# Capped attention and a rational MLP on one core: the row sums of four head pairs made together, tanh written from PSUM to SBUF, and another order of the products

## The chip, the cores and the metric

The kernel runs on one core of a Trainium2 chip. The metric is the device time of one execution in microseconds (us). The time before is 669.54 us, the median of three runs (669.12 to 669.55). A measurement of this kernel can tell a change of about 0.2% (1.3 us) from none.

## The reference

Attention with capped scores over 4 batches, 12 heads, 448 positions and a head dimension of 64, then an MLP whose activation is a rational function, all in float32:

```python
scores = q @ k.T / sqrt(64)
scores = cap * tanh(scores / cap)                       # cap = 30
attn = exp(scores - max(scores)); attn /= sum(attn) + 1e-9
x = (attn @ v)                                          # [1792, 768] over all heads
h = x @ w_in                                            # [1792, 2048]
P = a0 + a1*h + a2*h**2 + a3*h**3
Q = 1 + |b0|*|h| + |b1|*h**2
out = (P / (Q + 1e-6)) @ w_out                          # [1792, 768]
```

With a cap of at most 40 the kernel takes no maximum: the exponent is bounded (`self.bounded` is true here, and only this branch runs).

## The kernel before

**Attention.** The 48 heads are worked as 24 pairs, p = 0 to 23. The scores stand transposed, keys on the partitions and 448 queries in the free dimension. A pair has three full tiles of 128 keys, n = 0 to 2, each with both heads side by side (128 x 896); the last 64 keys of an even pair and of the odd pair behind it share a fourth tile, n = 3, which is made with the odd pair. So two pairs have seven tiles. Each tile is made by three products of split operands (`scores`, L417) into one of three pairs of PSUM banks (`PS`, in the order rows ps_127, ps_128, ps_129). ScalarE then takes tanh in place in PSUM (`softmax`, L429) and exp from PSUM to a tile in SBUF (`exp`, L447). There are six such SBUF tiles for n = 0 to 2 (`etiles`) and two for n = 3. VectorE adds the three exp tiles of a pair into one tile (`es`, L453, four buffers).

Then TensorE makes, per pair, the products with V (`pv`, L501, into the PSUM bank pv for even pairs and mi for odd ones), and per two pairs the products of the shared tile (`pv_tails`, L518) and the row sums (`norm`, L546). `norm` multiplies `es` and the n = 3 tile by columns of ones. Each of its products gives 32 rows of the result, so four of them lie side by side in the array: two rounds of four, into mi. VectorE copies the sums out (L550), four small DMAs fold them, VectorE takes reciprocals (L559, L560), one DMA writes them to DRAM and two DMAs spread them over 64 partitions. VectorE multiplies the output of each pair by them (`xout`, L579). All these DMAs go through GpSimd's queue, those of the last two `norm`s through SyncE's.

Before a pair's scores its keys and queries are transposed on TensorE (`prep_k`, L338 and L340, `prep_q`, L361), and VectorE (in the first pair ScalarE too) splits them out of PSUM with four instructions (L345, L346, L376, L379). This is done two pairs ahead.

**MLP.** `stage1` (L803, then L788) multiplies x by a block of w_in, `rational` (L834 to L847) works on ScalarE and VectorE, `stage2` (L873) multiplies by w_out. x is split into two parts (`split_x`, L590 and L591), half of it while attention still runs and half of it behind.

**The order.** Nothing runs in program order as such: `op` records each piece of work with a cost, the keys that it reads and writes, and a priority, and `Plan.flush` places them by these costs into one fixed order per engine. On the chip every engine then follows its own order and waits on semaphores. `visits(p)` gives the program order of a pair's pieces, which sets the priorities:

```python
            if p == 0:
                return [s0, s1, s2, (k, 1), (q, 1)]
            if p == 1:
                return [s0, s1, (k, 2), s2, t, (q, 2), (pv, 0), (k, 3), (q, 3)]
            if not p % 2:
                return [s0, s1, s2, (pv, p - 1), (tails, p - 1), *new]
            sums = (norm, p // 2 - 1)
            if p == P1 - 1:
                return [s0, s1, (pv, p - 1), sums, s2, t]
            return [s0, s1, (pv, p - 1), s2, t, *new, sums]
```

Here s0 to s2 and t are `scores` and `softmax` of the tiles, and `new` is the transposing for pair p + 2. The text calls TensorE's work on consecutive tiles of scores a scores block, the transposes of a pair a transpose block, and two pairs' work (from one odd pair's V block to the next) a period.

Of the kernel before, what the change touches and what calls it, by code (L numbers as in the profile page):

```python
# [22 lines left out]
RING, ARENA_F, ARENA_R = 3072, 15104, 24576  # L23
NE = 6
X_AT, RING_V32 = 5376, 2816
# [19 lines left out]
WARM2 = (2, 1, 3)  # L45
Q_ACT = ()
# [7 lines left out]
E_SC = 0  # L54
SC_NS = 615
# [4 lines left out]
D_NS = 1430  # L60
E_W = 10
# [181 lines left out]
class Body:  # L243
# [151 lines left out]

    def slot(self, p, n):

        return (1, 2, 0, 1)[n] if p % 2 else n
# [42 lines left out]
    def exp(self, p, n, src, sk, e, ek):  # L441
# [9 lines left out]
        es, ks = self.es[p % 4], [("es", p % 4)]  # L451
# [76 lines left out]
    def norm(self, k):  # L528
# [7 lines left out]
        DB, sc, dn = self.DB, self.SC[k % 2], self.dn[k % 2]  # L536
        es = [self.es[(2 * k + x) % 4] for x in range(2)]
# [11 lines left out]
        self.op(PE, D_NS + SHAPE_NS, sums, [("es", (2 * k + x) % 4) for x in range(2)] + [tk, "ones"], [dk, "turn"])  # L549
# [19 lines left out]

    def last_norm(self, k):  # L570

        return k + 1 == self.B * self.NP // 2
# [9 lines left out]
    def split_x(self, m, kc):  # L582

        nc = self.nc
        XH, XL = (t[m][kc].rearrange("p (b t) -> p b t", b=2) for t in (self.XH, self.XL))
# [7 lines left out]
    def attention(self):  # L593
# [7 lines left out]
        for t, x in [(self.ones, 1.0)] + [(self.half[j][64 * y:64 * y + 64], float(j == y)) for j in range(2) for y in range(2)]:  # L601
# [9 lines left out]
        def norm(k):  # L611
            self.norm(k)
            todo.extend([None] * (1 - len(todo)) + [2 * k, 2 * k + 1])

# [6 lines left out]
        def visits(p):  # L621
# [19 lines left out]
            return [s0, s1, (pv, p - 1), s2, t, *new, sums]  # L641
# [128 lines left out]
    def stage1(self, u, between=None):  # L770
# [10 lines left out]
        if between:  # L781
            for x, ts in enumerate(parts):
                def run(ts=ts):
                    w = wi().rearrange("p s (k f) -> p s k f", f=128)
                    for kc in range(KC):
                        h, lo = (t[m][kc][:, ts] for t in (self.XH, self.XL))
# [9 lines left out]
        for kc in range(KC):  # L796
            h, lo = ([t[m][kc][:, ts] for ts in parts] for t in (self.XH, self.XL))
# [180 lines left out]
    def memory(self):  # L978
# [42 lines left out]
        for l, nm, num, w in ((self.es, "es", 4, 896),):  # L1021
            for n in range(num):
                t, o = take(w)
                keys("A", o, ((nm, n), w))
                l.append(t.rearrange("p (a b) -> p a b", b=448))
# [9 lines left out]
        t, o = take(96)  # L1035
        keys("A", o, ("ones", 96))
        self.ones, *self.half = (t[:, 32 * x:32 * x + 32] for x in range(3))
        for n in range(2):
            t, o = take(56, 32)
# [59 lines left out]

        base[0] = ARENA_R - 3 * 896  # L1100
# [12 lines left out]
        for m in range(2):  # L1113
            for kc in range(self.KC):
                for l, nm in ((self.XH, "xh"), (self.XL, "xl")):
                    t, o = take(2 * self.S, dt=F32R)
                    keys("M", o, ((nm, m, kc), 2 * self.S))
                    l[m].append(t)
# [4 lines left out]
        for n, at, l, name in ((0, 0, self.wi, "w_in"), (0, 1, self.wi, "w_in"), (1, 0, self.wi, "w_in"), (1, 1, self.wo, "w_out")):  # L1123
            self.rings[(name, len(l))] = [("rv", n, 0), ("v32", n, 0), ("v32", n, 1)]
            at *= 2 * self.DM
            wt(l, name, 2 * 10 ** 6 + 4 * (RING * n + at), lambda n=n, at=at: self.shared(n)[:, at:at + 2 * self.DM])

# [12 lines left out]
    def run(self):  # L1140
        tc = self.tc
        self.rslot, self.made, self.later = {}, set(), {}
        with ExitStack() as ctx:
# [11 lines left out]
            self.dn = dp.tile([2, 4, self.S], F32, name="dn")  # L1155
            self.gtile = lambda dt: T("etiles", [128, 896 * (NE + 2)], dt)
            self.etiles = self.gtile(F32)
            self.ringtile = lambda n, dt: T(f"ring{n}", [128, RING], dt)
# [14 lines left out]
def attention_rational_mlp(ctx: ExitStack, tc: tile.TileContext, q, k, v, cap, moe_w_in, moe_w_out,  # L1173
# [4 lines left out]
    with tc.manual_schedule():  # L1178
# [21 lines left out]
        for n in (4, 5, 3):  # L1200
# [61 lines left out]
```

## Time and profile before

| | us |
|---|---|
| median of three runs | 669.54 |
| the profiled execution | 666.99 |
| its span, first to last instruction | 665.0 |
| TensorE busy | 652.5 (98%) |
| VectorE busy | 547.0 (82%) |
| ScalarE busy | 442.9 (67%) |
| GpSimd busy | 96.3 (14%) |
| mean granted TensorE clock | 0.998 of full |

The profile is of one execution, and its engines' busy times include the pipelined ends of matmuls, so that TensorE's 98% hides waits that are shorter than such an end. Where a product starts is exact, so the text measures blocks from the start of one to the start of the next. Attention's first scores start at 8.59 us, its last TensorE work ends at 192.39 us; the MLP takes the rest.

### The profile page before, as it was taken

To read this page: it belongs to the slowest core of one execution; us is meant where nothing else is said; L and a number is where in the kernel's file an instruction comes from. 1 tells how busy PE (TensorE), PEld (TensorE's weight loads), DVE (VectorE), ACT (ScalarE), POOL (GpSimd) and SP (SyncE) were. 2 spreads that over 40 slices of the span, in tenths; PEclk is the share of its full clock that TensorE was granted. 3 is DMA by queue.
4 is the path that set the end of the run, shared out by engine and by line. 5 is a ranking of instruction groups with operands and counts; after the bars stand their busy time and mean duration, and the time that the engine had idled before them with its cause. 6 is when DMAs were issued, how large, how long until landed. Compare 5 with 4: busy or idle time off the path is not lost.

```text
span 665.0 us, 9868 instructions
## 1 busy us (share of the span) xinstructions
PE 652.5 (98%) x3852; PEld 541.4 (81%) x3852; DVE 547.0 (82%) x677; ACT 442.9 (67%) x531; POOL 96.3 (14%) x159
## 2 busy tenths in 40 slices
PE   7999999999999999999999999999999999999996
PEld 4555555555458899999999999999999999999996
DVE  4779899998959988887996996899699789959753
ACT  5798989998958866765576455657645665754460
POOL 4023323323200000021012002101200210110030
PEclk9999999999999999999999999999999999999999
DMA  7746766764131332276148316714831671482086
GB/s 176 177 125 168 163 159 159 148 131 108 35 106 29 118 143 70 72 143 130 41 92 178 84 49 119 143 50 89 178 87 48 123 139 52 88 174 44 1 138 200
DMA packets 79895, 74.44 MB, mean 112 GB/s; under 512 B 49376, under 2 KB 68064, under 8 KB 79840
## 3 DMA queue, kind: packets, MB, share of 16 engines
q1 hardware_dynamic: 68240, 48.68, 26.1%
q0 software_dynamic: 10448, 24.80, 22.4%
q8 instruction: 32, 0.52, 0.3%
q10 hardware_dynamic: 1152, 0.25, 0.2%
q14 instruction: 23, 0.19, 0.1%
HBM read 47.98 MB, written 25.65 MB: 111 GB/s over the span
## 4 chain that ended last, share of the span: by engine, by line
PE 86%; ACT 6%; DVE 3%; DMA 2%; issue 1%; SPq 0%; ACTq 0%; DVEq 0%
PE ps L788 31%; PE ps L873 17%; PE mi L873 9%; PE pv L873 9%; PE ps L417 8%; PE mi L501 4%; PE pv L501 3%; ACT etiles L447 2%; PE mi L546 2%; ACT ps L429 2%; PE ps L338 1%; PE pv L518 1%; PE ps L361 1%; ACT arena_r L590 1%; DMA arena_f<-in_k_dram 1%
## 5 line engine op out<-in xcount | busy, mean ns | idle before, releaser
L788 PE MATMUL ps<-arena_r,ring 128*128 128x512 f32 (+1 forms) x1008 | 210.8, 363 | 0.0
L788 PEld LDWEIGHTS ps<-arena_r,ring 128*128 128x128 f32 x1008 | 182.2, 188 | 19.2
L290 POOL DMA_DIRECT2D out_dram<-arena_f x49 | 42.4, 865 | 418.8 <-ACT arena_f L900 415.2
L873 PE MATMUL ps<-arena_r,etiles 128*128 128x384 f32 x462 | 89.4, 334 | 0.1
L429 ACT ACTIVATE ps<-ps 128x896 f32<-128x896 f32 x84 | 74.3, 907 | 19.3 <-PE ps L417 18.8
L447 ACT ACTIVATE etiles<-ps,acap 128x896 f32<-128x896 f32 x84 | 82.4, 1011 | 1.1
L873 PEld LDWEIGHTS ps<-arena_r,etiles 128*128 128x128 f32 x462 | 80.9, 188 | 0.4 <-ACT arena_f L900 0.4
L873 PE MATMUL mi<-arena_r,etiles 128*128 128x384 f32 x231 | 77.2, 336 | 0.0
L873 PE MATMUL pv<-arena_r,etiles 128*128 128x384 f32 x231 | 77.0, 335 | 0.0
L417 PE MATMUL ps<-arena_r 64*128 64x448 f32 x576 | 70.8, 379 | 4.6 <-DVE arena_r L346 2.0
L417 PEld LDWEIGHTS ps<-arena_r 64*128 64x128 f32 x576 | 50.5, 184 | 29.5 <-ACT etiles L447 6.8
L834 ACT ACTIVATE arena_f<-ps,b 128x896 f32<-128x896 f32 x32 | 32.3, 1009 | 52.2 <-PE ps L788 52.0
L734 ACT ACTIVATE arena_f<-arena_f 128x768 f32<-128x768 f32 x32 | 29.3, 915 | 45.9 <-DMA arena_f<-in_moe_w_out_dram 31.4
L846 ACT CAST etiles<-arena_f 128x896 fp32r<-128x896 f32 x32 | 30.3, 947 | 42.9 <-DVE arena_f L845 42.9
L838 DVE SCALAR_TENSOR_TENSOR arena_f<-arena_f,bab 128x896 f32<-128x896 f32 x32 | 36.8, 1150 | 20.6 <-ACT arena_f L835 20.5
L843 DVE SCALAR_TENSOR_TENSOR arena_f<-arena_f,one 128x896 f32<-128x896 f32 x32 | 36.7, 1148 | 11.3 <-ACT arena_f L841 11.3
L873 PEld LDWEIGHTS pv<-arena_r,etiles 128*128 128x128 f32 x231 | 43.3, 188 | 0.6
L873 PEld LDWEIGHTS mi<-arena_r,etiles 128*128 128x128 f32 x231 | 43.3, 188 | 0.6
L873 PE MATMUL ps<-ring,etiles 128*128 128x384 f32 x210 | 42.0, 334 | 0.0
L847 DVE TENSOR_TENSOR etiles<-arena_f,etiles 128x896 fp32r<-128x896 f32 x32 | 34.8, 1089 | 6.8 <-ACT etiles L846 6.5
L836 ACT ACTIVATE arena_f<-ps,a 128x896 f32<-128x896 f32 x32 | 35.3, 1103 | 3.5 <-DVE arena_f L844 3.5
L873 PEld LDWEIGHTS ps<-ring,etiles 128*128 128x128 f32 x210 | 36.9, 188 | 0.0
(125 smaller groups left out, 1089.5 us busy)
## 6 DMA issues: line engine op xcount, KB each, us to landing
out_dram<-arena_f POOLq DMA_DIRECT2D x49, 384.0 KB, 6.0
arena_f<-in_moe_w_out_dram SPq DMA_DIRECT2D x16, 768.0 KB, 5.2
arena_f<-in_moe_w_in_dram SPq DMA_DIRECT2D x16, 768.0 KB, 4.8
out_dram<-arena_f SPq DMA_DIRECT2D x13, 384.0 KB, 2.6
ring<-in_q_dram SPq DMA_DIRECT2D x44, 112.0 KB, 4.2
arena_r<-dn POOLq DMA_DIRECT2D x20, 224.0 KB, 4.8
ring<-in_k_dram SPq DMA_DIRECT2D x33, 128.0 KB, 4.3
ring<-in_v_dram SPq DMA_DIRECT2D x11, 384.0 KB, 3.9
```

Source lines behind the costliest of these rows:

```text
L290: self.op(eng, (625 if local else 450) if eng == SP else 1050, lambda: e.dma_start(out, in_, **accum), r, w, nbytes=nbytes, **kw)
L417: m = nc.tensor.matmul(self.PS[i][:, j, 0:448], st[r], mv[r], start=y == 0, stop=y == len(ops) - 1)
L429: self.op(ACT, act_ns(896, True), lambda: nc.scalar.activation(ps, ps, AF.Tanh), ["table"], pk)
L447: self.op(ACT, act_ns(size, sk[0][0] == "ps", 1), lambda: nc.scalar.activation(e, src, AF.Exp, scale=acap), sk + ["table"], [ek])
L501: m = nc.tensor.matmul(po[64 * j:64 * j + 64, 0:448], raw["v"][:, 2 * x + j, 64 * c:64 * c + 64], tiles[c][0][:, j], start=c == 0, stop=False)
L788: r = nc.tensor.matmul(po[:, ts], w[:, y, kc], mv, start=kc == 0 and z == 0, stop=kc == KC - 1 and z == 2)
L834: self.op(ACT, act_ns(n, True, 1), lambda: T.activation(Bt, h, AF.Abs, scale=b[:, 0:1]), hk, bk)
L836: self.op(ACT, act_ns(n, True, 2), lambda: T.activation(A, h, AF.Identity, scale=a[:, 3:4], bias=a[:, 2:3]), hk, ak)
L838: self.op(DVE, dve_ns(n, 1), lambda: stt(Bt, C, bab[:, 1:2], Bt, ALU.mult, ALU.add), ck + ["bab"], bk)
L843: self.op(DVE, dve_ns(n, 1), lambda: stt(Bt, Bt, one, C, ALU.add, ALU.mult), ck, bk)
L847: self.op(DVE, dve_ns(n), lambda: V.tensor_tensor(GL(), A, f32(GH()), ALU.subtract), ak + K("gh", ig), K("gl", ig))
L873: r = nc.tensor.matmul(po[n][:, 0:384], st, mv[:, 384 * n:384 * n + 384], start=(y == 0 and x == 0), stop=(y == self.NCH - 1 and x == 2))
```

## The change

Five edits.

1. `norm4` makes the row sums of four pairs at once. Its stationary operands have a one in column 0 or column 1 (`unit`) or the two halves of the partitions in columns 0 and 1 (`both`), so that the two sums of one head position stand in two rows of one block of 32. Three rounds of four products take the place of twice two rounds. It runs at p = 5, 9, 13, 17 and 21; the last two `norm`s stay as they were. One copy, four folding DMAs, two reciprocal instructions and one DMA to DRAM serve four pairs, then four spreading DMAs follow.
2. Two more `es` tiles (`NES` = 6), which share their memory with two tiles of the second half of x (`SHARED_X`).
3. tanh reads PSUM and writes the exp tile in SBUF; exp works there in place. tanh gets a priority six places earlier (`E_TANH`).
4. `visits`: an odd pair's four tiles of scores stand together, its V products come last; an even pair's transposes stand ahead of its V products. The first two pairs are ordered otherwise, with two times four products on zeros (`fill`).
5. One first load (of keys) goes ahead of two (of queries) on ScalarE's queue.

```diff
+FILL = (4, 4)
+E_TANH = 6
@@ softmax
+        self.op(ACT, act_ns(896, True), lambda: nc.scalar.activation(e, ps, AF.Tanh), pk + ["table"], [ek], early=E_TANH)
         if self.bounded:
-            self.op(ACT, act_ns(896, True), lambda: nc.scalar.activation(ps, ps, AF.Tanh), ["table"], pk)
-            self.exp(p, n, ps, pk, e, ek)
-        else:
-            self.op(ACT, act_ns(896, True), lambda: nc.scalar.activation(e, ps, AF.Tanh), pk + ["table"], [ek])
+            self.exp(p, n, e, [ek], e, ek)
@@ norm4
+        def sums():
+            for last in range(3):
+                for y in range(2):
+                    for j in range(2):
+                        h = 32 * (2 * y + j)
+                        st, mv = (self.both, tails[y][0]) if last == 2 else (self.unit[last], self.es[es[2 * y + last][1]])
+                        m = nc.tensor.matmul(D[h:h + 32], st, mv[:, j], start=not last, stop=last == 2)
+            return m
...
+        for h in range(4):
+            self.dma(POOL, sc[16 * h:16 * h + 16], DB[32 * h:32 * h + 2].rearrange("o (s t) -> o s t", s=8), ["db"], keys[h:h + 1])
...
+        self.dma(POOL, dn.rearrange("h (s t) -> (h s) t", s=8), sc, keys, [("dn", k // 2 % 2)])
+        for y in range(2):
+            i = (k + y) % len(self.BC)
+            for j in range(2):
+                h = 2 * (2 * y + j)
+                self.dma(POOL, f32(self.BC[i])[64 * j:64 * j + 64].rearrange("p x t -> p (x t)"),
+                         dn[h:h + 2].rearrange("x t -> (x t)").unsqueeze(0).broadcast_to([64, 2 * self.S]),
+                         [("dn", k // 2 % 2)], [("bc", i, x, j) for x in range(2)])
@@ visits
             if p == 0:
-                return [s0, s1, s2, (k, 1), (q, 1)]
+                return [s0, s1, (k, 1), (q, 1), s2, (self.fill, FILL[0])]
             if p == 1:
-                return [s0, s1, (k, 2), s2, t, (q, 2), (pv, 0), (k, 3), (q, 3)]
+                return [s0, (self.fill, FILL[1]), s1, (k, 2), s2, t, (q, 2), (k, 3), (q, 3), (pv, 0)]
             if not p % 2:
-                return [s0, s1, s2, (pv, p - 1), (tails, p - 1), *new]
+                return [s0, s1, s2, *new, (pv, p - 1), (tails, p - 1)]
             sums = (norm, p // 2 - 1)
             if p == P1 - 1:
                 return [s0, s1, (pv, p - 1), sums, s2, t]
-            return [s0, s1, (pv, p - 1), s2, t, *new, sums]
+            four = [(norm4, p // 2 - 2)] * (p % 4 == 1)
+            return [s0, s1, s2, (self.scores, p, 3), *four, (self.softmax, p, 3), *new, (pv, p - 1)]
@@ first loads
-        for n in (4, 5, 3):
+        for n in (3, 4, 5):
             nc.scalar.dma_start(*first[n][1:3])
```

**In the middle of attention, TensorE.** An odd pair before (L417 scores, L501 products with V, L338 to L361 transposes, L546 row sums; ps_127 to ps_129 are the three PSUM pairs):

```order
L417 MATMUL ps_128<-arena_r 128x448 x6
L417 MATMUL ps_129<-arena_r 128x448 x6
L501 MATMUL pv<-etiles,ring_140 64x448 x6
L417 MATMUL ps_127<-arena_r 128x448 x6
L417 MATMUL ps_128<-arena_r 128x448 x12
L338 MATMUL ps_129<-ident,ring_141 128x128 x3
L340 MATMUL ps_129<-ident,ring_141 128x128
L361 MATMUL ps_129<-ident,ring_141 128x112 x4
L546 MATMUL mi<-arena_f 32x448 x4
L546 MATMUL mi<-etiles,arena_f 32x448 x4
```

The same place in the changed kernel, in a pair with `norm4` (L429 scores, L594 row sums, L343 to L366 transposes, L511 products with V):

```order
L429 MATMUL ps_128<-arena_r 128x448 x6
L429 MATMUL ps_129<-arena_r 128x448 x6
L429 MATMUL ps_127<-arena_r 128x448 x6
L429 MATMUL ps_128<-arena_r 128x448 x12
L594 MATMUL mi<-arena_f 32x448 x8
L594 MATMUL mi<-etiles,arena_f 32x448 x4
L343 MATMUL ps_129<-ident,ring_142 128x128 x3
L345 MATMUL ps_129<-ident,ring_142 128x128
L366 MATMUL ps_129<-ident,ring_142 128x112 x4
L511 MATMUL pv<-etiles,ring_141 64x448 x6
```

The two scores blocks became one, the V products moved from inside them to the end, and the row sums (twelve products every second odd pair, where eight stood in every odd pair) moved ahead of the transposes.

**At the start, TensorE.** Pair 1 and the first transposes for pairs 2 and 3, before (ring_141 holds the keys and queries of pairs 2 and 3):

```order
L417 MATMUL ps_127<-arena_r 128x448 x6
L417 MATMUL ps_128<-arena_r 128x448 x12
L361 MATMUL mi<-ident,ring_141 128x112 x4
L501 MATMUL pv<-etiles,arena_f 64x448 x6
L338 MATMUL ps_129<-ident,ring_141 128x128 x3
L340 MATMUL ps_129<-ident,ring_141 128x128
L361 MATMUL ps_129<-ident,ring_141 128x112 x4
```

And in the changed kernel:

```order
L429 MATMUL ps_127<-arena_r 128x448 x6
L429 MATMUL ps_128<-arena_r 128x448 x12
L366 MATMUL mi<-ident,ring_142 128x112 x4
L343 MATMUL ps_129<-ident,ring_142 128x128 x3
L345 MATMUL ps_129<-ident,ring_142 128x128
L366 MATMUL ps_129<-ident,ring_142 128x112 x4
L511 MATMUL pv<-etiles,arena_f 64x448 x6
```

The transposes for pair 3 moved ahead of pair 0's products with V.

**Where attention ends, TensorE.** The last scores, V products, tails and sums, and the MLP's first products in the changed kernel (L858 is `stage1`, L528 the tails, L556 `norm`):

```order
L429 MATMUL ps_128<-arena_r 128x448 x12
L858 MATMUL ps_127<-arena_r,ring_1748 128x512
L858 MATMUL ps_127<-arena_r,ring_1748 128x384
...
L511 MATMUL mi<-etiles,ring_142 64x448 x6
L528 MATMUL pv<-etiles,ring_142 64x448
L528 MATMUL mi<-etiles,ring_142 64x448
...
L556 MATMUL ps_129<-extra,arena_f 32x448 x4
L556 MATMUL ps_129<-etiles,arena_f 32x448 x4
L858 MATMUL ps_127<-arena_r,ring_1748 128x512
```

Before, all of `stage1` stood behind the last `norm`:

```order
L417 MATMUL ps_128<-arena_r 128x448 x12
L501 MATMUL mi<-etiles,ring_141 64x448 x6
L518 MATMUL pv<-etiles,ring_141 64x448
L518 MATMUL mi<-etiles,ring_141 64x448
...
L546 MATMUL ps_129<-arena_f 32x448 x4
L546 MATMUL ps_129<-etiles,arena_f 32x448 x4
L803 MATMUL ps_127<-arena_r,ring_1764 128x512
```

Six products of the MLP now stand between attention's last scores and its last V products, since PSUM pair ps_127 comes free with tanh. From ScalarE's table load and VectorE's `bab` on, the orders of ScalarE and VectorE are the same in both kernels.

## Rows read from the trace of the kernel before

**Rows 1.** The page, part 1: engine, busy us (share), instructions.
```profile
PE 652.5 (98%) x3852; PEld 541.4 (81%) x3852; DVE 547.0 (82%) x677; ACT 442.9 (67%) x531; POOL 96.3 (14%) x159
```
**Rows 2.** Windows: stretch, length, busy us of each engine (instructions), granted clock, DMA, GB/s.
```profile
30.26:192.39 162.13, 160.97 (x1207) 84.84 (x1207) 145.28 (x220) 144.78 (x163) 47.15 (x88) 1.00 0.57 134
192.39:665.00 472.61, 466.74 (x2500) 441.72 (x2496) 384.53 (x429) 278.23 (x345) 42.37 (x49) 1.00 0.45 101
```
**Rows 3.** Timeline of PE, one period without a wait: start us, length us.
```profile
146.37 2.48 PE L501 MATMUL mi<-etiles,ring 128*64 128x448 f32 x12
148.78 0.59 PE L518 MATMUL pv<-etiles,ring 64*64 64x448 f32 x1
...
150.66 1.49 PE L417 MATMUL ps<-arena_r 64*128 64x448 f32 x12
152.08 2.48 PE L501 MATMUL pv<-etiles,ring 128*64 128x448 f32 x12
154.48 2.09 PE L417 MATMUL ps<-arena_r 64*128 64x448 f32 x18
156.50 0.55 PE L338 MATMUL ps<-ident,ring 128*128 128x128 f32 x3
...
157.47 0.96 PE L546 MATMUL mi<-arena_f 128*32 128x448 f32 x8
158.25 0.94 PE L546 MATMUL mi<-etiles,arena_f 128*32 128x448 f32 x8
159.12 2.09 PE L417 MATMUL ps<-arena_r 64*128 64x448 f32 x18
161.14 1.35 PE L501 MATMUL mi<-etiles,ring 128*64 128x448 f32 x6
```
**Rows 4.** Timeline of PE: period starts, one wait, attention's end.
```profile
40.98 2.48 PE L501 MATMUL mi<-etiles,ring 128*64 128x448 f32 x12
...
114.75 1.49 PE L417 MATMUL ps<-arena_r 64*128 64x448 f32 x12 [0.38 <-ACT etiles L447]
...
175.91 2.48 PE L501 MATMUL mi<-etiles,ring 128*64 128x448 f32 x12
...
192.39 30.01 PE L803 MATMUL ps<-arena_r,ring 128*128 128x512 f32 x144
```
**Rows 5.** The start: timelines of PE and DVE, and a window as in rows 2.
```profile
25.16 0.87 PE L417 MATMUL ps<-arena_r 64*128 64x448 f32 x6 [1.15 <-DVE arena_r L379]
...
30.26 1.48 PE L417 MATMUL ps<-arena_r 64*128 64x448 f32 x12
...
22.64 0.69 DVE L345 CAST arena_r<-ps 128x512 fp32r<-128x512 f32 x1
...
12.00:14.00 2.00, 0.38 (x2) 0.21 (x2) 2.00 (x5) 2.00 (x3) 0.00 (x0) 1.00 0.75 170
```
**Rows 6.** ACT: timeline in the period of rows 3, then groups (busy us, mean ns).
```profile
160.03 1.71 ACT L429 ACTIVATE ps<-ps 128x896 f32<-128x896 f32 x2 [0.84 <-PE ps L417]
161.64 1.91 ACT L447 ACTIVATE etiles<-ps,acap 128x896 f32<-128x896 f32 x2
163.42 0.94 ACT L429 ACTIVATE ps<-ps 128x896 f32<-128x896 f32 x1
...
L429 ACT ACTIVATE ps<-ps 128x896 f32<-128x896 f32 x84 | 74.3, 907 | 19.3 <-PE ps L417 18.8
...
L447 ACT ACTIVATE etiles<-ps,acap 128x896 f32<-128x896 f32 x84 | 82.4, 1011 | 1.1
...
L835 ACT ACTIVATE arena_f<-ps 128x896 f32<-128x896 f32 x32 | 29.1, 910 | 0.0
...
L841 ACT ACTIVATE arena_f<-arena_f,eb 128x896 f32<-128x896 f32 x32 | 33.6, 1050 | 0.5
```
**Rows 7.** Behind attention: a window as in rows 2, and timeline of PE's weight loads.
```profile
200.00:240.00 40.00, 39.95 (x204) 36.21 (x203) 39.51 (x43) 31.81 (x38) 0.00 (x0) 1.00 0.23 81
...
226.62 2.06 PEld L873 LDWEIGHTS ps<-arena_r,etiles 128*128 128x128 f32 x12 [0.37 <-ACT arena_f L900]
```

More of the change, by code (lines that the diff above doesn't have):

```diff
@@ L394, in busy, with fill @@
                     [], [("ps", 2), "turn"])
+    def fill(self, n):
+        z = self.io["arena_r"][:, 0:512]
+        for _ in range(n):
+            self.op(PE, 213, lambda: self.nc.tensor.matmul(self.PS[0][:, 1], z[:, 0:128], z, start=True, stop=True),
+                    [], [("ps", 0), ("psb", 0), "turn"])
     def slot(self, p, n):
@@ L547, in sums @@
             return m
-        self.op(PE, D_NS + SHAPE_NS, sums, [("es", (2 * k + x) % 4) for x in range(2)] + [tk, "ones"], [dk, "turn"])
+        self.op(PE, D_NS + SHAPE_NS, sums, [("es", (2 * k + x) % NES) for x in range(2)] + [tk, "ones"], [dk, "turn"])
         self.op(DVE, dve_ns(448), lambda: nc.vector.tensor_copy(DB, D), [dk], ["db"], early=E_EV)
@@ L600, in attention @@
                 self.op(POOL, 300, fn, [], [("kz", n)])
-        for t, x in [(self.ones, 1.0)] + [(self.half[j][64 * y:64 * y + 64], float(j == y)) for j in range(2) for y in range(2)]:
+        for t, x in [(self.ones, 1.0)] + [(self.half[j][64 * y:64 * y + 64], float(j == y)) for j in range(2) for y in range(2)] + [
+                (t, 0.0) for t in (*self.unit, self.both)] + [(self.unit[x][:, x:x + 1], 1.0) for x in range(2)] + [
+                (self.both[64 * x:64 * x + 64, x:x + 1], 1.0) for x in range(2)]:
             self.op(POOL, 150, lambda t=t, x=x: nc.gpsimd.memset(t, x), [], ["ones"])
@@ L613, in norm, with norm4 @@
             todo.extend([None] * (1 - len(todo)) + [2 * k, 2 * k + 1])
+        def norm4(k):
+            self.norm4(k)
+            todo.extend([None] * (1 - len(todo)) + [2 * k + x for x in range(4)])
         def tile(p, n):
@@ L1020, in memory @@
         self.es = []
[L1021 to L1025, printed above, removed]
+        for n in range(4):
+            t, o = take(896)
+            keys("A", o, (("es", n), 896))
+            self.es.append(t.rearrange("p (a b) -> p a b", b=448))
         self.DB, o = take(448)
@@ L1034, in memory @@
             self.et32.append(self.etiles[:, o:o + 896].rearrange("p (a b) -> p a b", b=448))
-        t, o = take(96)
-        keys("A", o, ("ones", 96))
+        t, o = take(192)
+        keys("A", o, ("ones", 192))
         self.ones, *self.half = (t[:, 32 * x:32 * x + 32] for x in range(3))
+        self.unit, self.both = [t[:, 96 + 32 * x:128 + 32 * x] for x in range(2)], t[:, 160:192]
         for n in range(2):
-            t, o = take(56, 32)
+            t, o = take(56, 64)
             keys("A", o, ([("sc", n, h) for h in range(4)], 56))
@@ L1098, in memory @@
             self.qring[n] = (S.rearrange("p (s n) -> p s n", s=3), QL)
+        for n in range(NES - 4):
+            keys("A", 4 * 10 ** 6 + 4 * 896 * n, (("es", 4 + n), 896))
+            self.es.append(self.extra[:, 896 * n:896 * n + 896].rearrange("p (a b) -> p a b", b=448))
+        assert base[0] <= ARENA_R - 3 * 896
         base[0] = ARENA_R - 3 * 896
@@ L1126, in memory, with extras @@
             wt(l, name, 2 * 10 ** 6 + 4 * (RING * n + at), lambda n=n, at=at: self.shared(n)[:, at:at + 2 * self.DM])
+    def extras(self):
+        if "x" not in self.later:
+            self.later["x"] = self.extratile(F32R)
+        return self.later["x"]
     def gtiles(self):
```

42 lines of the change are left out of this document (33 added, 9 removed).

## The prediction

> **What bounds the kernel now.** The page's first part comes first: TensorE is busy for 98% of the span, every other engine has room [rows 1]. Since a matmul's pipelined end counts as busy, that is an upper bound, and the windows by stage and the timeline of TensorE tell the rest. In both stages, attention from pair 3 on and the MLP, the granted clock is 1.00, the 2.4 GHz level, so there is no clock to win [rows 2]. In attention TensorE's weight loads fill only 84.84 of 162.13 us, against 441.72 of 472.61 us in the MLP [rows 2]: attention is where TensorE's time goes into something other than full products.
>
> The timeline shows what [rows 3]. A period without a wait runs from the odd pair's V block at 146.37 to the next at 161.14, which is 14.77 us, in nine blocks, each measured from its start to the next one's: V products 2.41, tails 0.91 and transposes 0.97 (1.88 together, split by the later transposes), two tiles of scores 1.42, V products 2.40, three tiles 2.02, transposes 0.97, row sums 1.65, three tiles 2.02. Two tiles cost 1.42 and three 2.02, so a tile costs 0.60 and every scores block 0.22 more, for the change from another shape of the array. In the row sums the second round starts 0.78 behind the first and takes 0.87 to the next block's start.
>
> Then the waits. From pair 3's scores (30.26) [rows 5] to attention's end (192.39) [rows 4] I compare with the blocks. 30.26 to 40.98 takes 10.72 where the blocks give 10.48 (1.42 + 2.40 + 2.02 + 0.97 + 1.65 + 2.02). The nine periods to 175.91 take 134.93 where 9 x 14.77 = 132.93. The rest takes 16.48 where the blocks give 15.78 (2.41 + 0.91 + 1.42 + 2.40 + 1.65 + 2.02 + 2.41 + 0.91 + 1.65). So TensorE waits 0.24 + 2.00 + 0.70 = 2.94 us in all, mostly for a PSUM pair that ScalarE's exp still reads, as at 114.75 (the bracket gives the idle time before the row and what ended it) [rows 4]. Attention is TensorE's block time, with little waiting; what counts is how many blocks the change removes.
>
> **The change, part by part.**
>
> *Row sums of four pairs.* Twice two rounds become three. Two sums cost 2 x 1.65 = 3.30; one more round on a sum costs 1.65 + 0.78 = 2.43. That saves 0.87 us, five times (p = 5 to 21): 4.35 us. Bounds: 0.78 each if the third round costs 0.87 (3.9 us), and 0.89 (4.45 us). VectorE is relieved of a copy and two small instructions five times; I count nothing for it, since it only waits less. The folding and spreading DMAs on GpSimd's queue fall from 14 for two sums to 9; the loads of V's last rows queue behind them, but are issued a group of four heads ahead. The result is needed no earlier than VectorE's order puts `xout`, some 8 us behind the reciprocals, which is about the distance before.
>
> *One scores block in an odd pair.* In ten pairs (3 to 21) two blocks become one of five tiles' length (the shared tile counts double), 5 x 0.60 + 0.22: one change of shape less, 10 x 0.22 = 2.2 us. Bounds: 0, if the transposes now standing next to V products pay it back, and 2.4. All other blocks keep their number.
>
> *tanh into SBUF.* tanh keeps its source, PSUM; an instruction of the same size that writes SBUF from PSUM took 910 ns against tanh's 907 [rows 6]. exp now reads SBUF: with an operand of the same kind that form took 1050 ns against 1011. Over 84 tiles that is 0.25 + 3.3 us on ScalarE, which is busy for 144.78 of 162.13 us there [rows 2]; it lies beside TensorE's work, and were that cover gone it would cost at most these 3.5 us. The Trainium skill's page "ScalarE: Activation LUTs" (Step-by-step: what each stage is for) says that ScalarE writes PSUM with less latency than SBUF, which speaks against the edit. It gives no figure, so its sum would be a little below mine; the trace shows 3 ns for it.
>
> In return a PSUM pair comes free after tanh, where it was held through exp: of two tiles in a row the first gets its exp 1.61 us after its tanh began, and the next tanh comes after another 1.78 [rows 6]. So a tanh in a row takes 0.80 and an exp 0.89, by the groups' means 0.93 from SBUF. I follow a period: scores start at 0; tanh takes the first tile at 0.91 (159.12 to 160.03) [rows 3, 6], the second behind it, and after an exp the third. The shared tile needs the first one's bank at 2.0, and has it at 1.7. The transposes at 3.2 need the second one's, free at 2.5. The next scores, at 6.6 without row sums (3.22 + 0.97 + 2.41), find everything free but the transposes' bank; VectorE, at some 0.6 us per instruction (its four took 2.4 us from 22.64 to the tile at 25.16) [rows 5], empties it by 6.7 where it is needed at 8.0. The other half takes 2.02 + 0.97 + 2.41 + 0.91 = 6.3. ScalarE needs 7 x (0.80 + 0.93) = 12.1 us of this period of 12.9, and of 15.3 in one with row sums. There the shared tile's tanh has a new wait: it writes a buffer that the row sums read, until 3.2 + 2.4 = 5.6. ScalarE's order has the exps of the odd pair's three tiles ahead of it, so little is held up behind it, and the spare 3 us cover that. So most of the 2.94 us of waits could go, but VectorE, busy for 145.28 of 162.13 us [rows 2], and ScalarE's share of weight and x splitting stay, in a shorter stage. I leave 2.5 us of waits: a gain of 0.44, with bounds of +2.9 (none left) and -2.5 (waits of 5.4 us).
>
> *The start.* Before, pair 2's third tile waits 1.15 us until 25.16 for VectorE, which works on pair 3's transposes from 22.64 on [rows 5]. Those transposes now stand ahead of pair 0's V products, so VectorE can begin 2.4 us earlier, a V block's length. Then the wait of 1.15 goes, and with it the second start of a scores block (0.22): 1.4 us, so that pair 3's scores come at about 28.9 in place of 30.26. Bounds: 0, if ScalarE, which works without a pause here (2.00 of 2 us), sets the pace anyway, and 2.0, with the 0.6 us of one VectorE instruction as an allowance for the earlier load of keys. The eight products on zeros take some 1.7 us of idle TensorE; where TensorE was busy for only 0.38 of 2 us the granted clock still read 1.00 [rows 5], so I count no gain for them, and no cost, as ScalarE is behind them.
>
> *Attention's end.* The weight loads of the MLP's first second-stage products wait only 0.37 us for a chain over VectorE, which is busy for 39.51 of 40 us there [rows 7]. That chain starts at the second last `norm`, so it moves with TensorE. The last `norm` comes 1.2 us later against TensorE's work, since six MLP products stand ahead of it, and two more `xout` fall behind attention: I take -0.3, with bounds of -1.2 and +0.37. The MLP itself stays as it is.
>
> **The sum.** 4.35 + 2.2 + 0.44 + 1.4 - 0.3 = 8.1 us. The profiled execution's 666.99 (span 665.0 and 2.0 around it) becomes 658.9. The runs' median is 2.55 above that execution, so I forecast 669.54 - 8.1 = 661.4, in its own range 659.0 to 665.0 (ends taken partly together). A measurement tells 0.2%, 1.3 us, from no change.
>
> **Rivals.**
>
> *ScalarE sets the pace.* The half of the periods without row sums leave ScalarE 0.8 us; one weight or x split there (some 0.9 us each, as long as a tanh) or a tanh and exp of the same tile in a row uses it up, and TensorE waits for a bank. In five such periods at 1 us each the gain falls to 3 us: 666.5. For it speaks that ScalarE's work grows while the stage shrinks; against it that only tanh now holds a bank. Chance 0.14.
>
> *Slower, by the exp tiles.* tanh used to need only PSUM; now it needs a free SBUF tile, which V products and VectorE's sums of two pairs before must have read. In my walk V products end 0.9 us before an even pair's tanh wants the tile, and VectorE's sums some 3 us. From the point where VectorE trails exp by more than 3 us, every pair's tanh waits, and TensorE behind it. At 0.8 us in each of 20 pairs that is 16 us: 669.5 - 8.1 + 16 = 677.4. Before, VectorE's sums mostly followed exp within 2 us. Chance 0.06.
>
> *No change.* If attention ends earlier, but the chain behind it does not move, since it is VectorE's own backlog that holds it, TensorE waits those 8 us at the first second-stage products: 669.5. Against it: the chain goes back through DMAs to the row sums, and VectorE has less work. Chance 0.04.
>
> *All waits go* and the start gains 2 us: 657.5 or less. Chance 0.03.
>
> **How the numbers follow.** My forecast has the remaining 0.73. The range from 658.5 to 666.5 takes in nearly all of the forecast and most of the first rival, and leaves out the others. Faster by over 0.2%: 0.73 + 0.14 + 0.03 = 0.90; within 0.2%: 0.04; slower: 0.06.
>
> **What the changed profile would show.** If I am right: five blocks of row sums of 2.4 us, odd pairs' scores blocks of 3.2 us, two periods together of about 28.3 us where they took 29.5, pair 3's scores near 28.9, TensorE's last attention block near 184, and then the MLP with the same blocks as before. I am wrong if the row sums take 3 us, if scores wait for tanh or tanh for VectorE, or if TensorE waits by microseconds at the first second-stage products.

## The result, and the profile after

The changed kernel takes 660.97 us in the median of five runs (658.80 to 662.77), the kernel before 669.55 us in five runs beside it: a ratio of 0.9869, 95% interval 0.9848 to 0.9891, or 8.6 us less. The forecast was 661.4. A second set of five runs gave 659.97 (659.55 to 661.07) and a ratio of 0.9868 (0.9845 to 0.9891).

Two executions of the changed kernel have a profile, one of 662.77 us (span 660.7) and one of 659.97 us (span 657.8). The second is a median one and is called the middle execution; the first shows a loss of its own, which comes last. The profiled execution of the kernel before took 666.99 us, 2.6 us below its median, so between profiles the middle execution is 7.0 us shorter, and 7.2 us in span.

The first part of the middle execution's page, against [rows 1], and its windows by stage, against [rows 2]: the start, attention from pair 3's scores to the last row sums, and the rest.

```profile
PE 647.1 (98%) x3820; PEld 542.5 (82%) x3820; DVE 541.6 (82%) x662; ACT 442.2 (67%) x531; POOL 84.7 (13%) x141
```
```profile
8.00:28.96 20.96, 20.38 (x138) 12.07 (x139) 15.48 (x22) 17.81 (x20) 1.17 (x2) 1.00 0.84 194
28.96:187.16 158.20, 155.47 (x1176) 85.75 (x1172) 139.74 (x204) 144.41 (x164) 35.49 (x63) 1.00 0.56 139
187.16:657.80 470.64, 465.04 (x2494) 440.55 (x2490) 383.94 (x428) 277.84 (x344) 41.86 (x49) 1.00 0.44 101
```

Attention takes 158.20 us against 162.13, although 1.43 us of the MLP's products now lie inside it; the start is 1.30 shorter; the MLP is 1.97 shorter, most of it those same products. VectorE has 5.5 us less to do in attention, ScalarE as much as before.

TensorE's timeline in the middle execution, two periods, one with row sums of four pairs, against [rows 3] (start us, length us):

```profile
127.00 2.48 PE L511 MATMUL mi<-etiles,ring 128*64 128x448 f32 x12
...
130.32 3.38 PE L429 MATMUL ps<-arena_r 64*128 64x448 f32 x30
133.62 1.71 PE L594 MATMUL mi<-arena_f 128*32 128x448 f32 x16
...
136.02 0.55 PE L343 MATMUL ps<-ident,ring 128*128 128x128 f32 x3
...
136.99 2.48 PE L511 MATMUL pv<-etiles,ring 128*64 128x448 f32 x12
139.40 2.10 PE L429 MATMUL ps<-arena_r 64*128 64x448 f32 x18
141.42 0.55 PE L343 MATMUL ps<-ident,ring 128*128 128x128 f32 x3
...
142.40 2.48 PE L511 MATMUL mi<-etiles,ring 128*64 128x448 f32 x12
...
145.72 3.38 PE L429 MATMUL ps<-arena_r 64*128 64x448 f32 x30
...
152.41 2.09 PE L429 MATMUL ps<-arena_r 64*128 64x448 f32 x18
154.57 0.55 PE L343 MATMUL ps<-ident,ring 128*128 128x128 f32 x3
155.54 2.48 PE L511 MATMUL mi<-etiles,ring 128*64 128x448 f32 x12
```

Measured as before, from start to start: the row sums take 136.02 - 133.62 = 2.40 us, the five tiles' length of scores 3.30, an even pair's three tiles 2.02 (2.16 at 152.41, with a small wait). The two periods take 155.54 - 127.00 = 28.54 us, where two took 29.54 by their blocks. Behind 88 us nearly every block has this length. Most of the waits that are left stand ahead of it, while ScalarE and VectorE also convert the first weights. The table of TensorE's waits from 28 to 200 us (us in total, times, longest; L440 is tanh, L384 VectorE's last copy of queries out of the transposes' PSUM pair):

```profile
PE ps L343 <- ACT etiles L440: 1.4, 2, 0.8
PE ps L429 <- DVE arena_r L384: 1.1, 1, 1.1
```

### The profile page after: what moved, and what is told of

It reads as the page before. It is cut to its first block, busy times and chain, and to the rows that moved or that the text cites. A ratio compares the mean times of both kernels' runs of the same rounds, so it can differ in the third digit from the quotient of the medians.

```text
span 660.7 us, 9765 instructions
## 1 busy us (share of the span) xinstructions
PE 649.1 (98%) x3820; PEld 542.7 (82%) x3820; DVE 541.6 (82%) x662; ACT 442.2 (67%) x531; POOL 84.7 (13%) x141
## 4 chain that ended last, share of the span: by engine, by line
PE 86%; ACT 5%; DVE 4%; DMA 2%; issue 2%; SPq 0%; DVEq 0%; ACTq 0%
PE ps L843 31%; PE ps L928 17%; PE mi L928 9%; PE pv L928 9%; PE ps L429 7%; PE mi L511 4%; PE pv L511 3%; PE mi L594 2%; ACT etiles L440 2%; ACT etiles L457 2%; PE pv L528 1%; PE ps L343 1%; PE ps L366 1%; DMA arena_r<-dn 1%; DMA arena_f<-in_k_dram 1%
## 5 line engine op out<-in xcount | busy, mean ns | idle before, releaser
L843 PE MATMUL ps<-arena_r,ring 128*128 128x512 f32 (+1 forms) x924 | 207.6, 363 | 0.0
L843 PEld LDWEIGHTS ps<-arena_r,ring 128*128 128x128 f32 x924 | 167.7, 188 | 17.4
L440 ACT ACTIVATE etiles<-ps 128x896 f32<-128x896 f32 x84 | 74.6, 919 | 16.9 <-PE ps L429 14.2
L457 ACT ACTIVATE etiles<-etiles,acap 128x896 f32<-128x896 f32 x84 | 85.4, 1051 | 0.2
L429 PEld LDWEIGHTS ps<-arena_r 64*128 64x128 f32 x576 | 51.6, 186 | 26.4 <-ACT etiles L457 7.8
L429 PE MATMUL ps<-arena_r 64*128 64x448 f32 x576 | 68.2, 379 | 2.8 <-DVE arena_r L384 2.5
L889 ACT ACTIVATE arena_f<-ps,b 128x896 f32<-128x896 f32 x32 | 32.3, 1009 | 55.2 <-PE ps L843 55.0
```

What stands on the lines that cost most here:

```text
L429: m = nc.tensor.matmul(self.PS[i][:, j, 0:448], st[r], mv[r], start=y == 0, stop=y == len(ops) - 1)
L457: self.op(ACT, act_ns(size, sk[0][0] == "ps", 1), lambda: nc.scalar.activation(e, src, AF.Exp, scale=acap), sk + ["table"], [ek])
L843: r = nc.tensor.matmul(po[:, ts], w[:, y, kc], mv, start=kc == 0 and z == 0, stop=kc == KC - 1 and z == 2)
L889: self.op(ACT, act_ns(n, True, 1), lambda: T.activation(Bt, h, AF.Abs, scale=b[:, 0:1]), hk, bk)
```

## The experiments

Two theories stood against each other. **Block theory:** the parts are separate, each saves the blocks (or the small waits) that the prediction counted. **Bank theory:** the parts hang together, because each needs a PSUM pair to be free at a moment that another part provides. A third, the late-DMA theory, came from the first profile after. Each run had the kernel before beside it; differences between two changed kernels are differences of their ratios, times 669.5 us, and by the ratios' intervals each is known to about 2 us. Profiles are compared with the middle execution's.

**One part undone.** First the four parts of the changed kernel, one at a time.

Row sums of two pairs again:

```diff
-            four = [(norm4, p // 2 - 2)] * (p % 4 == 1)
+            four = [sums]
```

> The changed kernel with one edit: row sums go back to two pairs at a time (two rounds, every odd pair), at the same place behind the shared tile's products; order, tanh and start stay. Block theory (my term of 4.35 us): TensorE's block time returns, 5 x 0.87 = +4.35 us, so 665.3 against 660.97; the blocks read 1.65 us instead of 2.40, and no other block changes. Rival (DMA theory): the sums of four hand VectorE four pairs' results behind one chain of DMAs, and where that chain lands late VectorE and then TensorE stand still, as at 66 to 81 us of the changed kernel's profile; then undoing them gives part of it back, so only 0 to +2 us (661 to 663), with runs that lie within 1.5 us of each other instead of 4.

Measured: 667.14 us, ratio 0.9974 (0.9962 to 0.9987), 7.0 us above the changed kernel. The blocks read as expected (ten of 1.64 us for five of 2.40: 4.4 us). The rest is waiting: the scores blocks exceed their pure length by 4.6 us in sum, against 3.4 in the middle execution, and the MLP is 0.6 us longer, most of it at its first second-stage products, while pair 3's scores come 0.3 us earlier. That makes 5.9 of the 6.0 us between the two profiled spans (663.8 and 657.8). VectorE is the late one:

```profile
PE ps L429 <- DVE arena_r L384: 3.2, 4, 1.7
PE ps L928 <- ACT arena_f L955: 0.5, 1, 0.5
```

VectorE's timeline ahead of the longest of these waits (TensorE goes on at 70.44):

```profile
65.19 0.67 DVE L350 CAST arena_r<-ps 128x512 fp32r<-128x512 f32 x1
65.79 0.94 DVE L797 SCALAR_TENSOR_TENSOR arena_f<-arena_f 128x768 int32<-128x768 int32 x1
...
68.85 0.94 DVE L822 SCALAR_TENSOR_TENSOR arena_r<-arena_f,arena_r 128x768 fp32r<-128x768 f32 x1
69.71 0.67 DVE L384 SCALAR_TENSOR_TENSOR arena_r<-ps,c,arena_r 128x448 fp32r<-128x448 f32 x1
```

Instructions that convert weights (L797, L822) stand between the four that empty the transposes' PSUM pair. VectorE also has a copy and two small instructions more for every other sum; whether these, or only its other order, make it late is not shown. The rival, a smaller loss than the blocks, is refuted: the runs do not lie within 1.5 us of each other either, but spread over 3.1 us (665.68 to 668.81).

The order of before from pair 2 on:

```diff
-                return [s0, s1, s2, *new, (pv, p - 1), (tails, p - 1)]
+                return [s0, s1, s2, (pv, p - 1), (tails, p - 1), *new]
...
-            return [s0, s1, s2, (self.scores, p, 3), *four, (self.softmax, p, 3), *new, (pv, p - 1)]
+            return [s0, s1, (pv, p - 1), s2, (self.scores, p, 3), *four, (self.softmax, p, 3), *new]
```

> The changed kernel with one edit: from pair 2 on V products stand between the second and third tile of an odd pair again, and the transposes of an even pair behind V products and tails; sums of four, tanh into SBUF and the start stay. Block theory (my term of 2.2 us): one scores block more in ten odd pairs, 10 x 0.22 = +2.2 us, 663.2; the odd pair's scores read 1.4 and 2.0 us instead of one block of 3.3. Rival: the shape change saved there is paid elsewhere (transposes beside V products), 0 +- 0.5 us, 661.0.

Measured: 675.62 us, ratio 1.0100 (1.0080 to 1.0119), 15.5 us above the changed kernel and above the kernel before. Both theories of this run missed. TensorE's waits, and its timeline at one of the ten places:

```profile
PE ps L429 <- DVE arena_r L384: 10.6, 10, 1.2
```
```profile
114.81 0.55 PE L343 MATMUL ps<-ident,ring 128*128 128x128 f32 x3
...
115.79 1.49 PE L429 MATMUL ps<-arena_r 64*128 64x448 f32 x12
118.42 0.86 PE L429 MATMUL ps<-arena_r 64*128 64x448 f32 x6 [1.15 <-DVE arena_r L384]
```

An odd pair's transposes fill the PSUM pair that the next pair's third tile needs two tiles (1.4 us) later, and VectorE takes 2.4 us to empty it. The kernel before had its row sums (1.64 us) between them; with sums of four, which stand ahead of the transposes and only in every second odd pair, nothing is there but the V products of the new order. Each even pair's scores take 3.43 us in place of 2.02, ten times 1.41. The scores of an odd pair take 1.41 + 2.02 = 3.43 in two blocks against 3.30 in one: the change of shape that I had priced at 0.22 is worth 0.13 there. Between the profiles (673.8 and 657.8) attention is 12.1 us longer, these two terms (14.1 and 1.3) less the 3.4 us of waits that the middle execution has at other places, and the MLP 3.8 us, of which 2.9 are lost at its first second-stage products.

tanh back in PSUM:

```diff
-        self.op(ACT, act_ns(896, True), lambda: nc.scalar.activation(e, ps, AF.Tanh), pk + ["table"], [ek], early=E_TANH)
         if self.bounded:
-            self.exp(p, n, e, [ek], e, ek)
+            self.op(ACT, act_ns(896, True), lambda: nc.scalar.activation(ps, ps, AF.Tanh), ["table"], pk)
+            self.exp(p, n, ps, pk, e, ek)
```

> The changed kernel with one edit: tanh writes its PSUM pair in place again and exp reads PSUM; order, sums of four and start stay. Additive theory (my term of 0.44 us): +0.4 us, 661.4, at most +2.9. Rival (the parts hang together): five tiles' scores in one block need the first tile's bank back at 2.0 us, which with exp in PSUM comes at about 3.5 us (tanh from 0.9, exp at 2.5 to 3.4), so TensorE waits about 1.5 us in each of ten odd pairs, less where the block before ran late: +8 to +15 us, 669 to 676, which would be slower than the order of before needed; the wait would show as TensorE's scores idle on ScalarE's exp.

Measured: 691.73 us, ratio 1.0340 (1.0321 to 1.0359), 31.5 us above the changed kernel. The wait of the rival is there with its 1.5 us, and a second one of the same length, which it did not count, ahead of the even pairs' transposes:

```profile
PE ps L429 <- ACT etiles L459: 16.1, 11, 1.5
PE ps L343 <- ACT etiles L459: 13.6, 9, 1.5
```
```profile
103.62 1.48 PE L429 MATMUL ps<-arena_r 64*128 64x448 f32 x12 [1.50 <-ACT etiles L459]
...
112.03 0.55 PE L343 MATMUL ps<-ident,ring 128*128 128x128 f32 x3 [1.53 <-ACT etiles L459]
```

Both wait for the exp (L459) of a tile whose PSUM pair is wanted three tiles after it was filled. Together they are 29.7 of the 32.3 us between the profiles.

The old start:

```diff
-                return [s0, s1, (k, 1), (q, 1), s2, (self.fill, FILL[0])]
+                return [s0, s1, s2, (k, 1), (q, 1)]
...
-                return [s0, (self.fill, FILL[1]), s1, (k, 2), s2, t, (q, 2), (k, 3), (q, 3), (pv, 0)]
+                return [s0, s1, (k, 2), s2, t, (q, 2), (pv, 0), (k, 3), (q, 3)]
...
-        for n in (3, 4, 5):
+        for n in (4, 5, 3):
```

> The changed kernel with one edit: the visits of pairs 0 and 1, the first loads' order on ScalarE's queue and no products on zeros, all as before the change; the rest stays. Block theory (my term of 1.4 us): pair 3's scores start at about 30.3 instead of 28.9 and all behind it moves with them, +1.4 us, 662.4 (0 to +2.0). Rival: what starts earlier is caught up by ScalarE's or VectorE's backlog later, 0 +- 0.4 us, 661.0.

Measured: 662.54 us, ratio 0.9902 (0.9882 to 0.9923), 2.2 us above the changed kernel, with intervals that overlap. Pair 3's scores start at 29.79 instead of 28.96: 0.83 later, not 1.4. So the forecast of 662.4 was met by luck: of the 2.4 us between the profiles (660.1 and 657.8) 0.8 is the start, 0.5 lies in attention and 1.1 in the MLP, which this edit leaves alone. The rest of the 1.3 us that the changed kernel's start gains over the kernel before is not the order's; it comes with tanh, as the run with tanh alone shows.

**Half of the order undone**, the even pairs alone:

```diff
-                return [s0, s1, s2, *new, (pv, p - 1), (tails, p - 1)]
+                return [s0, s1, s2, (pv, p - 1), (tails, p - 1), *new]
```

> The changed kernel with one edit: in even pairs the transposes stand behind V products and tails again; odd pairs, sums of four, tanh and start stay. The number of blocks stays as it is. Block theory: 0 +- 0.4 us against 660.0 to 661.0. Bank theory: these transposes fill the bank that the odd pair's third tile needs 1.4 us later (behind V products before), while VectorE has two copies of V's results and four of the transposes to do, so TensorE waits about 1.1 us in each of ten pairs: +8 to +12 us, 669 to 673, with TensorE's scores idle on VectorE's last query copy.

Measured: 671.87 us, ratio 1.0044 (1.0029 to 1.0060), 11.7 us above the changed kernel, with the same blocks. TensorE's waits, then its timeline and VectorE's at one place:

```profile
PE ps L429 <- DVE arena_r L384: 12.8, 10, 1.5
```
```profile
91.87 1.49 PE L429 MATMUL ps<-arena_r 64*128 64x448 f32 x12
94.60 2.11 PE L429 MATMUL ps<-arena_r 64*128 64x448 f32 x18 [1.25 <-DVE arena_r L384]
```
```profile
91.01 0.62 DVE L535 COPY arena_f<-pv 128x448 f32<-128x448 f32 x1 [2.09 <-PE mi L528]
91.55 0.61 DVE L535 COPY arena_f<-mi 128x448 f32<-128x448 f32 x1
92.08 0.68 DVE L350 CAST arena_r<-ps 128x512 fp32r<-128x512 f32 x1
92.68 0.68 DVE L381 TENSOR_SCALAR arena_r<-ps,c 128x448 fp32r<-128x448 f32 x1
93.27 0.68 DVE L351 TENSOR_TENSOR arena_r<-ps,arena_r 128x512 fp32r<-128x512 f32 x1
93.87 0.67 DVE L384 SCALAR_TENSOR_TENSOR arena_r<-ps,c,arena_r 128x448 fp32r<-128x448 f32 x1
```

VectorE does two copies of V's results and four of the transposes, the last ends at 94.54, and the tile starts at 94.60. The bank theory, which gave 669 to 673 us, is shown by its place, its size and its count.

**One part alone**, on the kernel before. tanh into SBUF: the third edit of the change, with the visits, the sums and the first loads of before (`visits` as quoted ahead of the prediction).

> The kernel before with the tanh part alone: tanh writes SBUF and exp works there in place; visits, row sums of two pairs and the start stand as before the change. Block theory (my term of 0.44 us): -0.4 us against the kernel before beside it, about 668.8. If all of TensorE's waits were for PSUM that exp still reads: -2.9, 666.3. Rival (tanh waits for its SBUF tile): up to +8, 677. If the parts hang together, as the run with tanh back in PSUM showed (+31), this part is worth nothing by itself and everything in company: within 1 us of 669.2.

Measured: 666.54 us, ratio 0.9963 (0.9949 to 0.9977), 2.5 us below the kernel before: near the upper bound of 2.9. Between pair 3's scores and attention's end no scores block is longer than its pure length by more than 0.03 us any more; that stage takes 159.83 us against 162.13, and pair 3's scores come 0.63 earlier. Of these 2.9 us the MLP gives back 1.5, so that the spans differ by 1.4 (663.6 and 665.0). Its first second-stage products take 2.4 us longer, as they wait for ScalarE:

```profile
PE ps L927 <- ACT etiles L900: 1.2, 1, 1.2
PE ps L927 <- ACT arena_f L954: 0.6, 1, 0.6
```

Sums of four alone (the edits of the runs with the old start, the old pair order and tanh in PSUM together):

> The kernel before with the sums of four alone: tanh in PSUM, V products between the second and third tile of an odd pair, the old start; only that the sums must stand ahead of the shared tile's tanh, so they no longer stand between an odd pair's transposes and the next pair's tiles. Block theory: -4.4 us against the kernel before, 664.8. Bank theory: the third tile of the even pair needs the PSUM bank that holds the odd pair's transposes, 1.4 us after them, where VectorE needs 2.4 to 2.6 to empty it; about 1.06 us in each of ten pairs, -4.4 + 10.6 = +6, about 675: the sums of four would be a loss without the new order.

Measured: 677.70 us, ratio 1.0133 (1.0107 to 1.0159), 8.9 us above the kernel before. The even pairs' scores take 3.44 us (two of them more) instead of 2.02, as with the old pair order; where the sums stand ahead of the transposes the wait is for VectorE's last query copy, in the other pairs for an exp that still reads the second tile's PSUM pair:

```profile
PE ps L429 <- DVE arena_r L384: 5.8, 5, 1.2
PE ps L429 <- ACT etiles L459: 5.8, 5, 1.6
```

Alone, the largest term of my sum is a loss. Between the profiles (675.9 and 665.0) row sums take 4.4 us less, waits 14.0 more, of which about 2.0 go with a lower granted clock (shown at the end), and pair 3's scores come 1.3 us later.

**The late DMA.** In the first profile after, VectorE stood still for 4.63 us behind one transfer, and TensorE waited for it. VectorE's timeline, then POOL's queue (the transfer to DRAM is issued at 58.55; the bracket at 65.37 is the wait for its landing):

```profile
70.81 0.63 DVE L627 TENSOR_TENSOR arena_f<-arena_r,arena_f 128x448 f32<-128x448 f32 x1 [4.63 <-DMA arena_r<-dn]
```
```profile
58.55 0.55 POOL L295 DMA_DIRECT2D dn<-arena_f  x1
...
65.37 2.07 POOL L295 DMA_DIRECT2D arena_r<-dn  x4 [5.69 <-DMA dn<-arena_f]
```

Four runs asked whether that is worth mending: the changed kernel once more, the scaling (`xout`) one visit later, and the early weight loads one pair later, then both edits.

> The changed kernel, unchanged, so that the next three runs have it beside them on the same chip. Late-DMA theory: the profiled execution shows again a pause of VectorE of 2 to 5 us before pair 0's scaling by reciprocals, around 66 to 71 us, because the transfer that writes the reciprocals to DRAM (issued about 58.5) lands 3 to 7 us later behind a large weight load issued at 58.2; median 661.0, runs spread over 3 to 4 us. Rival (chance): the pause does not come back, its place changes from execution to execution.

```diff
-            todo.extend([None] * (1 - len(todo)) + [2 * k + x for x in range(4)])
+            todo.extend([None] * (2 - len(todo)) + [2 * k + x for x in range(4)])
```

> The changed kernel with one edit: after sums of four the scaling of results begins one pair visit later in VectorE's order (two empty places instead of one). Late-DMA theory: VectorE no longer stands behind the late transfer, so its pauses before that scaling (10.7 us in four in the changed kernel's profile) fall below 4 us and the 2.1 us that TensorE's scores wait for VectorE's query copies at 75 us go: -1 to -3 us against the changed kernel beside it, 658 to 660, with runs within 2 us of each other. Rival: VectorE merely meets its backlog later, or the later scaling pushes into attention's end: 0 +- 0.6 us, or +1.

```diff
-EARLY_AT = 3
+EARLY_AT = 4
```

> The changed kernel with one edit: the four early weight loads come one pair later (pairs 4, 6, 8, 10 instead of 3, 5, 7, 9) and their conversion with them, so no large load is issued just ahead of the reciprocals' transfer of pair 7's visit. Late-DMA theory: that transfer lands in 1.5 to 2.7 us instead of 6, VectorE's pause before the first scaling goes, -1 to -3 us, 658 to 660. Rival (the latency comes from the queue of key and query loads, which stay): landing still 4 us or more, 0 +- 0.6 us.

> Both edits of the two runs before it. Late-DMA theory: either removes the same loss, so both together give no more than the better one, -2 to -3 us, 658 to 659. Rival (two separate losses): the gains add up, -3 to -5 us, 656 to 658.

Measured: 659.97, 659.77, 659.74 and 659.88 us, ratios 0.9868, 0.9861, 0.9862 and 0.9870, each with an interval of about 0.0023 to either side. The pause recurs in the unchanged kernel at its place, 3.58 us long, with 3.4 us of waiting for the landing instead of 5.7 and 1.08 us of waiting on TensorE. Both edits remove that wait (the scores no longer wait for VectorE between 28 and 200 us; the wait for the landing is 3.3 us with the later scaling and 2.3 us with the later weights), but the gain, 0.1 to 0.2 us between medians, is below what can be told. Attention ends 1.0 to 1.5 us earlier in the three edited profiles, and the MLP takes 0.5 to 1.0 us longer. The theory names a real wait and overrates it: 1 to 3 us was the price in the one long execution, not in the median.

**The products on zeros** left out:

```diff
-FILL = (4, 4)
+FILL = (0, 0)
```

> The changed kernel without the eight products on zeros in TensorE's idle time at the start. My prediction: no gain and no cost, 0 +- 0.4 us, the granted clock reads 1.00 there with or without them. Rival (they hold the clock): the granted clock falls towards 0.5 somewhere between 8 and 26 us and up to 2 us are lost, 662 to 663.

Measured: 660.41 us, ratio 0.9862 (0.9836 to 0.9889): no difference. The granted clock reads 1.00 in each window from 8 to 28 us without them, and pair 3's scores even start at 28.38.

No run beats the changed kernel by more than its runs differ.

## Why the prediction was right, point by point

The median came within 0.4 us of 661.4 (the second set's within 1.4), and the direction and range held. The working was less right than the sum, and that the sum came so close is in part luck, as the last point says. Between the profile of before and the middle execution, spans 665.0 and 657.8, the terms are:

| term | forecast | measured |
|---|---|---|
| row sums | -4.35 | 5 x (3.30 - 2.40) = -4.5 |
| one scores block | -2.2 | 10 x (3.44 - 3.30) = -1.4 |
| waits | -0.44 | 2.94 became 3.4: +0.5 |
| start | -1.4 | 30.26 to 28.96: -1.3 |
| attention's end and MLP | +0.3 | 472.61 to 470.64, less 1.43 moved: -0.5 |
| sum | -8.1 | -7.2 |

- *Row sums of four pairs.* The third round was sized rightly (2.43 forecast, 2.40). "I count nothing for it" on VectorE may be wrong: with the new order, two-pair sums cost 7.0 us (6.0 between profiles), not 4.4, part of it because TensorE waits for a VectorE that has more to do and does it in another order.
- *One scores block.* This step failed by 0.8 us: 0.22 us was taken as the price of any change of shape, but here it is 0.13 to 0.14, as a block of five tiles' length takes 3.30 us, not 3.22. The prediction missed what the reorder is for. Its walk had VectorE empty the transposes' bank in time (by 6.7 us, wanted at 8.0), but gave no price to the V block that makes the room: every transpose block needs one behind it to give VectorE its 2.4 us. Undone by half it costs 11.7 us, undone whole 15.5.
- *tanh into SBUF.* The waits are the other term that failed, by 0.9 us: 2.5 us were forecast to stay, and 3.4 did, now for VectorE and for tanh, where before they were mostly for exp. And as a term, 0.44 us was near neither run: alone it gains 2.5, and in company it is what the five tiles in a row live on (31.5 us). My walk along a period held: five tiles find their banks free, and the even pairs' transposes wait 1.4 us for tanh in all.
- *ScalarE's pace* did not become the bound. tanh into SBUF takes 919 ns against 907 [rows 6], four times the 3 ns that I took, exp 1051 against a forecast 1050; together 4.4 us more on 84 tiles, beside TensorE's work. ScalarE's groups in the first profile (L457 is exp):

```profile
L457 ACT ACTIVATE etiles<-etiles,acap 128x896 f32<-128x896 f32 x84 | 85.4, 1051 | 0.2
L440 ACT ACTIVATE etiles<-ps 128x896 f32<-128x896 f32 x84 | 74.6, 919 | 16.9 <-PE ps L429 14.2 <-PE mi L594 2.4
```

 The Trainium skill's page "ScalarE: Activation LUTs" (Step-by-step: what each stage is for) prefers PSUM as the nearer destination; the 12 ns agree with it in direction and weigh nothing against the bank that comes free.
- *The start* came as forecast to 28.9, though about half of its 1.3 us belongs to tanh: by itself that part starts pair 3's scores 0.63 us earlier, since the wait for an exp at 15.22 us (0.42) goes.
- *Attention's end.* The chain behind the second-stage products moved with attention (0.47 us of waiting of the weight loads against 0.37 [rows 7]), so the rival "no change" is out. It does not move with every order: those products take 2.4 us longer with tanh alone and 2.9 with the old pair order. The row in the middle execution:

```profile
219.81 2.03 PEld L928 LDWEIGHTS ps<-arena_r,etiles 128*128 128x128 f32 x12 [0.47 <-ACT arena_f L955]
```

- The medians differ by 8.6 us and 9.3 us, the profiles by 7.0, since the profiled execution of before is 2.6 us below its median. The mean granted clock goes with the difference: of 49 executions of the kernel before that have one on record, the 32 at 0.996 or less have a median of 669.8 us, the 13 at 0.998 or more 667.6; the profiled one is at 0.998. The ten of the changed kernel are all at 0.997 or more. So about 2 us of the gain in medians stand beside a clock that the kernel before lacks in most executions. The prediction has no term for it: the blocks gave 7.2 us of the forecast 8.1, and what goes with the clock more than filled the gap. Where the longer executions lose it, and which part of the change keeps it, no trace of the kernel before shows.

The terms could be added only because all parts were there. The runs that take one away give +7.0, +15.5, +31.5 and +2.2 us, those that put tanh or the sums of four in alone -2.5 and +8.9; the order and the start have no run alone. The sum was near for the whole; no term is shown to be the worth of its part.

## What to carry to other kernels

A ledger of blocks tells the time of a whole change when every block then starts on time; it does not tell what each part is worth. Before adding up, walk each PSUM bank through a period: who fills it, who empties it and how long that takes, and how much other work stands between. Here 2.4 us of emptying want one V block behind every transpose block, and three tiles in a row want a bank back after tanh rather than after exp.

## What the hardware showed that was not expected

The first profile after lost more than its wait. Windows of that execution: ahead of the wait, the wait, the scores behind it, two rounds of row sums, the stretch at the lower clock, then on (columns as in [rows 2]); then the row that ends the row sums; in the last fence the scores behind the middle execution's shorter wait at the same place.

```profile
66.50:72.70 6.20, 5.74 (x40) 2.86 (x40) 1.89 (x3) 6.16 (x8) 2.00 (x4) 1.00 0.81 215
72.70:74.87 2.17, 0.04 (x2) 0.00 (x1) 2.17 (x5) 2.12 (x3) 0.12 (x1) 1.00 0.94 221
74.87:77.59 2.72, 2.72 (x19) 2.02 (x19) 2.72 (x5) 1.80 (x3) 0.00 (x0) 0.71 0.78 243
77.59:79.63 2.04, 2.04 (x14) 0.59 (x16) 2.04 (x3) 0.98 (x2) 0.00 (x0) 0.55 0.10 35
76.01:79.42 3.41, 3.41 (x22) 1.55 (x22) 3.41 (x5) 2.56 (x3) 0.00 (x0) 0.50 0.44 155
79.63:83.00 3.37, 3.37 (x30) 1.56 (x24) 2.60 (x5) 1.96 (x2) 1.04 (x2) 1.00 0.44 125
```
```profile
80.86 0.55 PE L343 MATMUL ps<-ident,ring 128*128 128x128 f32 x3
```
```profile
73.92:75.94 2.02, 2.02 (x19) 1.61 (x19) 2.02 (x5) 2.02 (x4) 0.00 (x0) 1.00 0.97 249
```

TensorE waited 2.13 us for VectorE. In the work that followed, the granted clock read 0.71 and then 0.55 (0.50, the 1.2 GHz level, in the stretch from 76.01), and 1.00 again from 79.63 on. The scores took 2.72 us instead of 2.02, the row sums 80.86 - 77.59 = 3.27 instead of 2.40. So the wait cost 2.13 + 0.70 + 0.87 = 3.7 us. Behind a wait of 1.08 us at the same place the clock stayed at 1.00. That is 1.05 + 1.57 = 2.6 us of the 2.9 us between the two spans, and a transfer that lands 2.3 us later in one execution than in another is behind it.

The length of one wait does not settle it. With the sums of four alone the clock read 0.50 behind a wait of 1.55 us that ended at 40.75:

```profile
41.47:44.88 3.41, 3.41 (x14) 1.41 (x12) 2.82 (x4) 3.38 (x5) 0.00 (x0) 0.50 0.38 80
```

With tanh back in PSUM some twenty waits of up to 1.5 us left it at 1.00 from 30 to 216 us. What decides between them, these runs do not show.
